# Attention decode with gradients on one core: dealing a head's cache rows to the partitions in another order, one transfer per head

## The chip, the core and the metric

The kernel runs on one core of a Trainium2 chip. TensorE (PE; its weight loads are listed as PEld), VectorE (DVE), ScalarE (ACT), GpSimd (POOL) and SyncE (SP) work side by side and meet through semaphores; 16 DMA engines carry data between HBM and the on-chip memory, whose 128 partitions hold the tiles. SP does no arithmetic here: it issues nearly all transfers, in the order written. The metric is the device time of one execution in microseconds.

## What is computed

A one-token attention step over a key and a value cache, mixed by a gate with a small dense network, and the gradients of the result by every input except the network's own (B_x). Sizes: D = 640, 32 heads of 128, 4096 cached positions, F = 1728, all in bf16.

```python
q = (x @ wq).reshape(1, 1, 32, 128)                 # one query per head
scores = einsum("bhqd,bhkd->bhqk", q, k_cache) * 128 ** -0.5
p = softmax(scores)
a = einsum("bhqk,bhkd->bhqd", p, v_cache).reshape(1, 1, 4096) @ wo
h = B_x @ w1 + b1
b = (h * tanh(softplus(h))) @ w2
g = sigmoid((x * gate_w).sum(-1))
out = g * a + (1 - g) * b
# returned: out and its gradients by x, k_cache, v_cache, wq, wo, w1, b1, w2, gate_w for grad_out
```

Each cache is 32 MB (32 heads x 4096 rows x 256 B). Both are read once, and a gradient of the same size is written for each. The gradient of a value row is the probability of its position times the head's output gradient; that of a key row is the score's gradient times the query. Softmax, sums and outer products run over a head's positions, and none of them depends on where a position stands.

## The kernel before

The heads are taken in 16 pairs (`NP`). For each pair `i` there is one tile of keys, `Kn`, and one of values, `Vn`: 128 partitions x 64 rows (`J`) x 128, 2 MB. Partitions 0 to 63 (`HP` = 64) hold the first head of the pair, 64 to 127 the second. The view at line 70 gives partition `a * 64 + q` the 64 consecutive cache rows of head `a` that begin at row `64 q`, which is one run of 16 KB in HBM. `load` (lines 106 to 111) brings such a tile with one DMA, or, for the first pair, with two DMAs of half of each partition's rows.

PE transposes the tiles (line 549, two bf16 values as one 32-bit word), ACT copies the transposes out of PSUM (line 560), and PE multiplies them with the query or the output gradient (line 575). From the row `x` (line 592) come scores and their gradients, with partition and row-in-partition as their two dimensions; maximum and sum over a head are taken across rows and the head's 64 partitions (lines 594 to 642). `dq_o` (line 675) goes through the natural tiles once more for the query's gradient and the head's output.

`out_part` (lines 651 to 666) makes a gradient tile on DVE in four outer products (`outer`, line 645, `JQ` = 16 rows of each partition at a time) and stores it: one DMA after the fourth (line 666), and for the first and the last pair one after every two (line 664). The tiles `o_sb` have two buffers, `Kn` and `Vn` two each; two of the last pairs' gradients go into `Kn` and `Vn` buffers that are no longer needed.

The order of the work is written out by hand, one engine's instructions in the order of the program: in step `i` the softmax of pair `i` runs, then transposes of pair `i + 1` between the outer products of pair `i`; the loads of pair `i + 2` are issued right after `dq_o(i)`, which is the last to read pair `i`. All these transfers are in SP's queue with the loads and stores of `wq` and `wo` (1280 KB for two groups of four heads and 640 KB for one; lines 129, 133, 415, 424) and of `w1` (lines 152, 887 and 888). `w2` is loaded and its gradient stored by an indirect DMA from POOL (lines 212 and 218) with one row of 20 KB for each of 108 partitions; the list `HOLES` names the 20 partitions that get none:

```python
HOLES = ((3, 5), (11, 13), (16, 20), (48, 52), (67, 69), (75, 77), (83, 85), (91, 93))
```

SP's DMAs use eight completion semaphores in turn, so each waits until the one eight before it has landed; a load waits besides for the last reader of its buffer, a store for DVE.

Of the kernel before, what the change touches and what calls it, by code (L numbers as in the profile page):

```python
# [16 lines left out]
def kernel(  # L17
# [24 lines left out]
    nc = tc.nc  # L42
    P = 128
    _, H, Sk, Dh = A_k_cache.shape
# [3 lines left out]
    J = 2 * Sk // P  # L48
    JU = J // 2
    NP = H // 2  # L50
    HP = P // 2
# [10 lines left out]
    for a, b in zip((0,) + tuple(b for a, b in HOLES), tuple(a for a, b in HOLES) + (P,)):  # L62
# [4 lines left out]
    TB = 8  # L67
    JQ = J // 4

    Kv, Vv, dKv, dVv = [t.rearrange("b (i a) (q j) d -> (b i) (a q) j d", a=2, j=J)  # L70
                        for t in (A_k_cache, A_v_cache, out_2, out_3)]
    wq_v = A_wq.rearrange("(rc r) c -> r rc c", r=P)
    dwq_v = out_4.rearrange("(rc r) c -> r rc c", r=P)
    wo4_v = A_wo.rearrange("(g p t) n -> g p t n", p=P, t=4)
# [31 lines left out]
    def load(tiles, src, name, i, parts=1):  # L106
        if i < NP:
            tiles[i] = kv_in.tile([P, J, Dh], BF16, name=name, tag=name)
            for k in range(parts):
                yield nc.sync.dma_start(tiles[i][:, k * J // parts:(k + 1) * J // parts, :],  # L110
                                        src[i][:, k * J // parts:(k + 1) * J // parts, :])

    def load_k(i):
        return list(load(kts, Kv, "Kn", i))

    def load_v(i):
        return list(load(vts, Vv, "Vn", i))
# [22 lines left out]
    dy_sb = mjunk[0:1, 0:D]  # L140
    nc.scalar.dma_start(dy_sb, dy_row)
    k0, v0 = load(kts, Kv, "Kn", 0, 2), load(vts, Vv, "Vn", 0, 2)
    next(k0)
    load_wqp(0)
# [499 lines left out]
    def outer(dst, col4, row, a, b):  # L644
        nc.vector.tensor_tensor(  # L645
            dst[:, a:b, :].rearrange("p j (k t) -> p j k t", t=4),
            row.rearrange("p (k t) -> p k t", t=4).unsqueeze(1).to_broadcast([P, b - a, Dh // 4, 4]),
            col4[:, a:b, :].unsqueeze(2).to_broadcast([P, b - a, Dh // 4, 4]), ALU.mult)

    o_t = {}  # L650

    def out_part(w, i, dst, col4, row, k):
        if k == 0:
            if w == "k" and i == NP - 2:
                o_t[w, i] = kv_in.tile([P, J, Dh], BF16, name="Kn", tag="Kn")
            elif w == "v" and i == NP - 1:
                o_t[w, i] = kv_in.tile([P, J, Dh], BF16, name="Vn", tag="Vn")
            else:
                o_t[w, i] = outs.tile([P, J, Dh], BF16, name="o_sb", tag="o_sb")
        outer(o_t[w, i], col4, row[:, i % 2 * Dh:(i % 2 + 1) * Dh], k * JQ, (k + 1) * JQ)  # L660
        if i in (0, NP - 1):
            if k % 2:
                js = slice((k - 1) * JQ, (k + 1) * JQ)
                nc.sync.dma_start(dst[i][:, js, :], o_t[w, i][:, js, :])
        elif k == 3:
            nc.sync.dma_start(dst[i], o_t.pop((w, i))[:])

    def dv_out(i, k):
        out_part("v", i, dVv, p4s[i], groups[i // 2]["do_row"], k)

    def dk_out(i, k):
        if i >= 0:
            out_part("k", i, dKv, ds4s[i], groups[i // 2]["qs_row"], k)
# [298 lines left out]
    g, i = NG - 1, NP - 1  # L972
# [102 lines left out]
```

## Time and profile before

| | |
|---|---|
| median of 3 runs | 405.23 us (404.2 to 407.51) |
| the profiled execution | 404.24 us, of which the profile's span is 402.4 |
| busy share of the span: PE, PEld, DVE, ACT, POOL | 73%, 51%, 69%, 56%, 7% |
| bytes moved | 164.54 MB, read and written in equal parts |
| SP's issues | 34 loads of `Kn` and `Vn` (30 of 2048 KB, 4 of 1024), 36 gradient stores (28 of 2048 KB, 8 of 1024), 27 others |
| granted TensorE clock, mean | 0.875 |

The page divides the span into 40 slices; a digit is the share of the slice in tenths. The DMA row is the mean over the 16 engines, and below it stand the GB/s that they moved. A packet is what an engine moves in one piece: for these tiles 16 KB, or 8 KB where a DMA takes half of each partition's rows. The trace also holds every packet's size and duration and the time of every semaphore increment; a DMA's completion semaphore goes up by 16, once for each DMA engine. The time to landing of a DMA is from its issue to the last of the 16.

### The profile page before, as it was taken

To read this page: it belongs to the slowest core of one execution; us is meant where nothing else is said; L and a number is where in the kernel's file an instruction comes from. 1 tells how busy PE (TensorE), PEld (TensorE's weight loads), DVE (VectorE), ACT (ScalarE), POOL (GpSimd) and SP (SyncE) were. 2 spreads that over 40 slices of the span, in tenths; PEclk is the share of its full clock that TensorE was granted. 3 is DMA by queue.
4 is the path that set the end of the run, shared out by engine and by line. 5 is a ranking of instruction groups with operands and counts; after the bars stand their busy time and mean duration, and the time that the engine had idled before them with its cause. 6 is when DMAs were issued, how large, how long until landed. Compare 5 with 4: busy or idle time off the path is not lost.

```text
span 402.4 us, 7413 instructions
## 1 busy us (share of the span) xinstructions
PE 294.7 (73%) x2886; PEld 204.3 (51%) x2886; DVE 278.7 (69%) x696; ACT 226.3 (56%) x484; POOL 27.5 (7%) x50
## 2 busy tenths in 40 slices
PE   3788889687859786685938887597957878396530
PEld 3556565465547463554626554464736655263220
DVE  3207257587849778877698957796697884459990
ACT  3465746577525955377445967659563865168030
POOL 9200005100000000000014000000000000010001
PEclk9898989999968999699979989689896999598555
DMA  7999999999999999999999999999999999999995
GB/s 273 433 420 416 420 415 433 417 422 396 428 377 401 385 416 430 421 417 430 427 430 428 420 417 429 405 423 423 430 413 393 425 415 430 401 425 428 397 419 226
DMA packets 20116, 164.54 MB, mean 409 GB/s; under 512 B 2456, under 2 KB 2457, under 8 KB 10905
## 3 DMA queue, kind: packets, MB, share of 16 engines
q1 hardware_dynamic: 18960, 159.62, 96.0%
q0 software_dynamic: 1088, 4.44, 2.7%
q8 instruction: 22, 0.36, 0.3%
q14 instruction: 14, 0.11, 0.1%
q10 hardware_dynamic: 32, 0.01, 0.0%
HBM read 82.44 MB, written 82.44 MB: 410 GB/s over the span
## 4 chain that ended last, share of the span: by engine, by line
DMA 53%; DVE 30%; PE 9%; ACT 4%; issue 2%; POOL 0%; POOLq 0%; ACTq 0%; DVEq 0%
DMA out_dram<-o_sb 51%; DVE o_sb L645 19%; PE tr L549 3%; ACT T L560 2%; DVE junk L508 1%; PE rw L575 1%; DMA Kn<-in_A_k_cache_dram 1%; DVE Vn L645 1%; DVE Kn L645 1%; DVE ds L637 1%; DVE junk L400 1%; DVE wq_p L410 1%; PE x L592 1%; PE do_ps L301 1%; PE mx L610 1%
## 5 line engine op out<-in xcount | busy, mean ns | idle before, releaser
L560 ACT COPY T<-tr 128x512 f32<-128x512 f32 x256 | 140.9, 592 | 108.8 <-PE tr L549 63.5
L549 PE MATMUL tr<-ident_f,Kn 128*128 128x128 f32 x512 | 85.0, 326 | 9.5 <-DMA Kn<-in_A_k_cache_dram 9.5
L645 DVE TENSOR_TENSOR o_sb<-do_row,p 128x2048 bf16<-128x2048 bf16 x60 | 69.4, 1219 | 29.7 <-DMA out_dram<-o_sb 29.7
L549 PE MATMUL tr<-ident_f,Vn 128*128 128x128 f32 x512 | 77.3, 284 | 12.4 <-ACT T L560 12.4
L549 PEld LDWEIGHTS tr<-ident_f,Kn 128*128 128x128 f32 x512 | 74.5, 174 | 16.1 <-issue 9.7
L645 DVE TENSOR_TENSOR o_sb<-qs_row,ds 128x2048 bf16<-128x2048 bf16 x60 | 73.0, 1223 | 13.3 <-DMA out_dram<-o_sb 13.3
L549 PEld LDWEIGHTS tr<-ident_f,Vn 128*128 128x128 f32 x512 | 54.4, 141 | 36.4 <-ACT T L560 22.3
L681 PE MATMUL rw<-Kn,dsm 128*8 128x512 bf16 x256 | 32.0, 394 | 3.4 <-DVE dsm L641 3.4
L681 PE MATMUL rw<-Vn,pm 128*8 128x512 bf16 x256 | 32.0, 394 | 0.0
L575 PE MATMUL rw<-T,doz 128*32 128x512 bf16 x256 | 21.2, 407 | 12.8 <-ACT T L560 12.8
L604 DVE TENSOR_REDUCE m<-sd 128x1 f32<-128x64 f32 x16 | 3.5, 216 | 32.2 <-ACT sd L599 32.2
L610 PE MATMUL mx<-ident_f,m_s 128*128 128x128 f32 x16 | 6.5, 408 | 25.6 <-DVE m_s L606 25.6
L400 DVE SCALAR_TENSOR_TENSOR junk<-wq_p,dq_bc 128x512 bf16<-128x512 bf16 x35 | 23.9, 684 | 0.0
L418 ACT ACTIVATE wo_g<-da_bc,o 128x640 bf16<-128x640 bf16 x28 | 23.8, 850 | 0.0
L592 PE MATMUL x<-ident_f,rw_sb 128*128 128x128 f32 x68 | 13.5, 331 | 13.0 <-ACT rw_sb L586 13.0
L575 PE MATMUL rw<-T,qz 128*32 128x512 bf16 x256 | 20.8, 401 | 0.2 <-ACT T L560 0.2
L592 PEld LDWEIGHTS x<-ident_f,rw_sb 128*128 128x128 f32 x68 | 8.6, 163 | 22.9 <-ACT rw_sb L586 22.9
L681 PEld LDWEIGHTS <-dsm 128*8 128x8 bf16 x256 | 11.1, 88 | 14.3 <-DVE dsm L641 8.2
L610 PEld LDWEIGHTS mx<-ident_f,m_s 128*128 128x128 f32 x16 | 2.6, 161 | 30.5 <-DVE m_s L606 30.5
L586 ACT COPY rw_sb<-rw 128x512 f32<-128x512 f32 x17 | 10.0, 591 | 11.2 <-PE rw L575 6.5
L599 ACT COPY sd<-x 64x128 f32<-64x128 f32 x32 | 8.3, 259 | 14.1 <-PE x L592 8.6
L516 POOL TENSOR_TENSOR mjunk<-ident_bf,dh_bf 128x96 bf16<-128x96 bf16 (+4 forms) x9 | 6.3, 728 | 136.3 <-DVE m L604 136.3
(183 smaller groups left out, 361.1 us busy)
## 6 DMA issues: line engine op xcount, KB each, us to landing
out_dram<-o_sb SPq DMA_DIRECT2D x27, 2048.0 KB, 14.7
Kn<-in_A_k_cache_dram SPq DMA_DIRECT2D x15, 2048.0 KB, 13.2
Vn<-in_A_v_cache_dram SPq DMA_DIRECT2D x15, 2048.0 KB, 17.6
out_dram<-o_sb SPq DMA_DIRECT2D x6, 1024.0 KB, 11.3
wq_p<-in_A_wq_dram SPq DMA_DIRECT2D x4, 1280.0 KB, 23.6
wo_g<-in_A_wo_dram SPq DMA_DIRECT2D x8, 640.0 KB, 20.2
out_dram<-wo_g SPq DMA_DIRECT2D x8, 640.0 KB, 12.8
out_dram<-wq_p SPq DMA_DIRECT2D x4, 1280.0 KB, 14.2
```

The costliest lines, as they stand in the source:

```text
L400: nc.vector.scalar_tensor_tensor(jq[:], in0=wqs[g][:, c, :], scalar=1.0, in1=groups[g]["dq_bc"][:], op0=ALU.mult, op1=ALU.mult, accum_out= ...
L418: nc.scalar.activation(wos[g][:, hh, :], da_bc[:], ACT.Copy, scale=groups[g]["o4"][:, hh:hh + 1])
L516: nc.gpsimd.tensor_tensor(mjunk[:, i * FCN:(i + n) * FCN].rearrange("p (a b) -> p a b", b=FCN), ident_bf[:, a:b].unsqueeze(2).to_broadcast ...
L549: nc.tensor.transpose(tp[:, t, :], words[:, t * P:(t + 1) * P], ident_f[:])
L560: nc.scalar.copy(TT[w, i, k][:, (3 - c) * (TB // 2):(4 - c) * (TB // 2), :], tp[:])
L575: nc.tensor.matmul(rw[32 * c:32 * (c + 1), :], lhsT=z[:, at:at + 32], rhs=Tb[:, c, par, :, :], start=first and par == 0, stop=last and par ...
L586: nc.scalar.copy(rw_sb[i][:].rearrange("p t r -> p (t r)"), rw[:])
L592: nc.tensor.transpose(xs[i][:, 3 - j, :], t[:, j, :], ident_f[:])
L599: nc.scalar.copy(sd[i][hs].rearrange("p s (k j) -> p k s j", k=2), v[hs, :, 8 + 4 * a:12 + 4 * a].rearrange("p j (k s) -> p k s j", k=2))
L610: nc.tensor.transpose(mx[:, 0:P], dgms.pop(i)[:].to_broadcast([P, P]), ident_f[:])
L645: nc.vector.tensor_tensor(dst[:, a:b, :].rearrange("p j (k t) -> p j k t", t=4), row.rearrange("p (k t) -> p k t", t=4).unsqueeze(1).to_br ...
L681: nc.tensor.matmul(rw[32 * c:32 * c + 8, :], lhsT=m[:, jb:jb + 4, :].rearrange("p q a -> p (q a)"), rhs=N[:, jb:jb + 4, :].rearrange("p j ...
```

## The change

Each head's 4096 rows are still cut into 64 runs of 64 rows (16 KB), one for each of the head's 64 partitions, but the runs are dealt in another order: partition `4 e + s` of a head (`e` from 0 to 15, `s` from 0 to 3) gets run `16 s + e`, where before partition `q` got run `q`. Four consecutive partitions thus hold runs that are 16 apart, and partitions 4 apart hold neighbouring runs. Keys, values and both gradients are dealt alike. A view with the pair's two heads in front would have needed one more dimension, so every transfer of a tile is made twice, once for each head: `flat` names the 64 partitions of a head in the tile, `dcols` the HBM side as 16 x 4 x bytes. The number of packets and their sizes stay, and no instruction on PE, DVE, ACT or POOL changes. SP issues 140 transfers of caches and gradients instead of 70.

```diff
-    Kv, Vv, dKv, dVv = [t.rearrange("b (i a) (q j) d -> (b i) (a q) j d", a=2, j=J)
+    Kv, Vv, dKv, dVv = [t.rearrange("b (i a) (s e j) d -> (b i) a e s (j d)", a=2, e=HP // 4, s=4)
                         for t in (A_k_cache, A_v_cache, out_2, out_3)]
+
+    def flat(t, a, js):
+        return t[a * HP:(a + 1) * HP, js, :].rearrange("p j d -> p (j d)")
+
+    def dcols(d, i, a, js):
+        return d[i, a, :, :, js.start * Dh:js.stop * Dh]
...
             for k in range(parts):
-                yield nc.sync.dma_start(tiles[i][:, k * J // parts:(k + 1) * J // parts, :],
-                                        src[i][:, k * J // parts:(k + 1) * J // parts, :])
+                js = slice(k * J // parts, (k + 1) * J // parts)
+                for a in range(2):
+                    nc.sync.dma_start(flat(tiles[i], a, js), dcols(src, i, a, js))
+                yield
...
             if k % 2:
                 js = slice((k - 1) * JQ, (k + 1) * JQ)
-                nc.sync.dma_start(dst[i][:, js, :], o_t[w, i][:, js, :])
+                for a in range(2):
+                    nc.sync.dma_start(dcols(dst, i, a, js), flat(o_t[w, i], a, js))
         elif k == 3:
-            nc.sync.dma_start(dst[i], o_t.pop((w, i))[:])
+            t = o_t.pop((w, i))
+            for a in range(2):
+                nc.sync.dma_start(dcols(dst, i, a, slice(0, J)), flat(t, a, slice(0, J)))
```

## The prediction, made before the changed kernel had run

> **What bounds the kernel now.** I read the page's slices first, since one core that moves 164.54 MB in 402.4 us is suspect of being bound by transfers, then the table of stretches, the chain of waits, the queues and issues, and last the trace's records of single packets and semaphore increments, which no view prints.
>
> The slices, the stretches (their columns: window, length, busy us of PE, PEld, DVE, ACT, POOL with counts, granted clock, DMA share, GB/s) and the chain:
>
> ```profile
> DMA  7999999999999999999999999999999999999995
> GB/s 273 433 420 416 420 415 433 417 422 396 428 377 401 385 416 430 421 417 430 427 430 428 420 417 429 405 423 423 430 413 393 425 415 430 401 425 428 397 419 226
> DMA packets 20116, 164.54 MB, mean 409 GB/s; under 512 B 2456, under 2 KB 2457, under 8 KB 10905
> q1 hardware_dynamic: 18960, 159.62, 96.0%
> ...
> DMA 53%; DVE 30%; PE 9%; ACT 4%; issue 2%; POOL 0%; POOLq 0%; ACTq 0%; DVEq 0%
> ```
>
> ```profile
> 40.00:200.00 160.00, 127.75 (x1333) 88.49 (x1331) 114.32 (x289) 94.17 (x206) 6.07 (x12) 0.94 1.01 415
> 200.00:360.00 160.00, 120.86 (x1165) 83.91 (x1163) 120.17 (x274) 99.35 (x209) 7.88 (x11) 0.87 1.01 419
> ```
>
> The DMA row is full in 38 of 40 slices, at 415 and 419 GB/s over the two middle stretches, while PE, DVE and ACT each have 32 us or more free in every 160. The best slices stand at 433 GB/s and none is above. The chain's other 47% is work between one transfer's end and the next issue; transfers already queued run beside it, or the DMA share would not be 1.01.
>
> ```profile
> out_dram<-o_sb SPq DMA_DIRECT2D x27, 2048.0 KB, 14.7
> Kn<-in_A_k_cache_dram SPq DMA_DIRECT2D x15, 2048.0 KB, 13.2
> Vn<-in_A_v_cache_dram SPq DMA_DIRECT2D x15, 2048.0 KB, 17.6
> ```
>
> A 2048-KB transfer follows its predecessor's landing by 4.9 us (K and V issued at 195.35 and 195.78 land at 208.54 and 213.42), so 14.7 us from issue to landing is about three tiles queued: the engines always have work waiting, and whatever makes a K/V transfer longer goes straight into the span.
>
> The packet records say what a packet costs. Median times are 84 ns for 2048 B, 196 for 5120, 309 for 8192, 611 for 16384, 761 for 20480 and 9 for the 4-B semaphore write. All six lie within 1 ns of 8 ns + bytes / 27.2 GB/s, loads and stores alike, in SP's queue and in POOL's. Of the 7,424 K/V packets of 16 KB 88% are within 1% of 611 ns. So each of the 16 engines runs at one fixed width, 27.2 GB/s, not at the pace of HBM.
>
> **The K/V share.** These 7,424 packets take 291.1 us of 16 engines' time and the 1,536 of 8 KB (pairs 0 and 15, moved in halves) 30.6: 321.7 us of the span are K/V traffic, of which only 7.6 + 0.9 = 8.5 us lie above the two medians.
>
> **The change, part by part.** *Order in HBM.* An engine's four rows of a head lie 256 KB apart instead of 16 KB, and what the 16 engines read at one time are 16 adjacent chunks instead of chunks 64 KB apart. Packets stay 16 KB (8 KB for the halves) with the same 8 ns each. The gain is bounded by the 8.5 us above the medians. The loss is bounded by the worst stretch of K/V packets, 110 to 120 us, at 376 GB/s against 16 x 611-ns packets' 429: if all K/V went so, 321.7 x (429/376 - 1) = 45 us. I take nothing: nine packets in ten have nothing to gain, and the neighbours of a chunk have no row that speaks against them.
>
> *More instructions.* 34 loads and 36 stores become 140, so 70 more issues at 0.34 us = 24 us on SP, which mostly waits (131 us for one kind of release alone) and has three tiles queued ahead; and 70 x 9 ns = 0.6 us of semaphore writes on each engine. SP reuses eight completion semaphores in turn, so a DMA waits for the landing of the one eight before it; eight half-tiles are still 8 MB, 19.5 us at the mean rate, against 14.7 us from issue to landing. Nothing is queued behind such a wait that the engines lack. PE's first transpose of a tile waits for two landings, both of which its one tile had before. DVE, ACT, POOL and PE keep their instructions; the sum over a head's rows does not care which partition has which row, since K, V, dK and dV are dealt alike. I take 0.6 us.
>
> *Half of the partitions at a time.* This decides. A tile's DMA has 128 partitions; now head 0's uses partitions 0 to 63, head 1's 64 to 127, one behind the other in the same queue. The trace of before has no big transfer on 64 partitions, so the price has two ends: nothing, if 27.2 GB/s is each engine's own width, or twice the time, if it is the width of the way into a group of partitions and two engines now share one. One transfer tells how partitions and engines belong together: the w2 load, whose row list leaves partitions 16 to 19 and 48 to 51 empty, and one or none of every other such 4 + 4. Of its 16 increments one comes 5.1 us before the next, the others lie within 1.9 us: one engine had nothing to do, so the blocks 16-19 and 48-51 are one engine's (seven to eight rows at 0.761 us are 5.3 to 6.1 us). Partitions 32 apart go to one engine, 64 apart to another: a division that looks like wiring, 16 ways of 27.2 GB/s with eight partitions each. A head on partitions 0 to 63 has eight of these ways, and if its 64 rows are dealt four to an engine, engines e and e + 8 meet in one. I take the upper end, because the constant is the same for both directions, both queues and all sizes, and the division follows the partitions.
>
> The Trainium skill's page "SBUF — State Buffer", section "Door 1: The DMA port swizzle (why `[64,N]` ≈ `[32,N]`)", says that partitions 0 to 63 reach eight of the 16 ports, and gives 196 GB/s against 328 for 1-MiB transfers on 64 and on 128 partitions; its next section adds that two transfers on the two halves don't overlap. By its ratio, 1.67, the K/V traffic would gain 216 us and the time be 620, an estimate from that page; no run here shows such a transfer yet.
>
> The sum by rows: at 13.6 GB/s a 16-KB packet takes 8 + 1205 = 1213 ns and an 8-KB one 610; 7,424 x 1213 / 16 + 1,536 x 610 / 16 = 562.8 + 58.6 = 621.4 us in place of 321.7: +300. The profiled execution took 404.2 (span 402.4 and 1.8 around it): 704. Two engines that meet lose less if one is ahead by part of a half tile (64 KB, 2.44 us). The tightest landing (the second half of K0) has all 16 within 0.40 us. The slowest pair sets when a buffer is released; pairs that gain a lead empty their queues, and both their engines start again together, so I take 0.1 us for it, 4% of 300, -12: 692 us, with 0.6 lost in rounding. The median of the three runs is 1.0 above the profiled one, too little to matter.
>
> **The rivals.** *Engines drift apart.* In mid-kernel the 16 landings of one DMA spread over 2 to 5 us (2.9 at 208.54, 5.7 at 345). If partners come to stand anywhere in the 4.9 us of a tile, they meet half of the time: +150, 555 us. For: the spread grows from 0.4 to over 5 us in the trace. Against: eight to ten of the 16 stay within 1 us, and one close pair is enough to hold the buffer. Between this and lockstep: 450 to 640.
>
> *The width is the engine's own.* Then nothing is lost; with 0.6 us of semaphores 405. For: the rate is the same whatever is moved. Against: so it would be with one way for each engine, and the w2 landings show engines tied to partitions.
>
> *Faster, by the order in HBM.* With the width the engine's own, the adjacent chunks could remove packets' excess: all of it gives 404.2 - 8.5 + 0.6 = 396, 2% faster. It decides from half of that on (4 us). For: the packets' excess is largest in 100 to 140 us, where hardly any other traffic runs, so it may be HBM's. Against: both conditions must hold, and there is little to win.
>
> *The order in HBM costs.* With the widths unshared, up to 45 us: 405 to 450, if chunks 256 KB apart on one engine slow it as packets in that worst stretch are slowed.
>
> **How the numbers follow.** Half ways in near lockstep 0.62 (640 to 740: partners 0.5 us apart take 20% off the 300; the top adds most of the 45 us); drift 0.18; order costs 0.05; no effect 0.06; faster 0.09. One per cent either way is about what a measurement of this kernel can tell from no change. Faster by over 1% is 0.09, within it 0.06, slower 0.85. The likeliest case alone ranges from 640 to 740; eight chances in ten need the drift as well, so 450 to 740.
>
> **What will show it.** In the changed kernel's slices DMA should stay at 9 with about 215 to 240 GB/s, PE and DVE digits falling to about half; 16-KB packets at 1.2 us rather than 0.61; issue to landing of a 1024-KB half no shorter than that of a whole tile now; wq and wo, still on 128 partitions, at their 84 and 196 ns unless they run beside a K/V packet. If packets mix 611 and 1213 ns, it is drift. If they stay at 611, the division into halves is free, and the sum's one large term is wrong; then the packets above 617 ns tell whether the order in HBM did anything.

## The result, and the profile after

The changed kernel takes 512.0 us (median of 4 runs, 504.8 to 517.7) against 404.7 for the kernel before (403.6 to 407.5): 1.247 times as long, 95% interval 1.240 to 1.254. That ratio counts only executions within 1.5% of their kernel's fastest, of the changed kernel those of 504.8 and 508.0 us; by the two medians it would be 1.265. Its profiled execution took 508.0 us, with a span of 506.3, 103.9 more than before.

The slices, the packets and the chain of waits of the changed kernel:

```profile
DMA  8999999999999899999999999999999999999994
GB/s 262 227 286 230 327 247 282 330 250 374 308 400 350 253 277 373 364 359 401 363 340 307 392 296 411 355 398 363 344 275 315 376 327 408 281 406 373 316 293 161
DMA packets 21236, 164.55 MB, mean 325 GB/s; under 512 B 3575, under 2 KB 3576, under 8 KB 12024
q1 hardware_dynamic: 20080, 159.62, 94.6%
...
DMA 65%; DVE 12%; PE 10%; SPq 6%; issue 2%; ACT 1%; ACTq 0%; POOLq 0%; POOL 0%; DVEq 0%
```

The DMA engines are as busy as before and carry a fifth less: 325 GB/s on average in place of 409. The bytes are the same, and the 1,120 additional packets are the 4-B semaphore writes (16 for each of 70 transfers). Two levels stand in the row: 227 to 330 in the first eight slices, then a restless 250 to 411. The table of stretches shows them in two lines (columns: window, length, busy us of PE, PEld, DVE, ACT, POOL with counts, granted clock, DMA share, GB/s):

```profile
20.00:110.00 90.00, 56.43 (x466) 38.97 (x466) 25.73 (x58) 35.49 (x78) 6.07 (x12) 0.77 1.02 276
110.00:480.00 370.00, 244.58 (x2376) 173.66 (x2374) 241.73 (x580) 184.48 (x393) 6.85 (x11) 0.80 0.99 348
```

Before, 20 to 110 us went at 419 GB/s and 110 to 380 at 416. The issues, with KB each and the median us to landing:

```profile
out_dram<-o_sb SPq DMA_DIRECT2D x54, 1024.0 KB, 19.1
Kn<-in_A_k_cache_dram SPq DMA_DIRECT2D x30, 1024.0 KB, 20.5
Vn<-in_A_v_cache_dram SPq DMA_DIRECT2D x30, 1024.0 KB, 22.3
```

Half a tile lands later than a whole one did. The packet records tell why. Of the 16-KB K/V packets 93% took up to 630 ns before; now 48% do, 13% take 1150 ns or more, and the rest lie between. From 65 to 110 us 4% take up to 630 ns and 61% 1150 or more, with a median of 1201 ns, which is the doubled packet; from 110 us on the median is 620. The K/V packets' time is 410.4 us of 16 engines' instead of 321.7 (+88.7), all packets' 495.2 instead of 399.2 (+96.0: the other packets take 7 us more too), and the rest of the 103.9 us, 8, is time in which engines had no packet.

### The profile page after: what moved, and what is told of

It is laid out like the page before. It is cut to its first block, busy times and chain, and to the rows that moved or that the text cites. A ratio compares the mean times of both kernels' runs of the same rounds, so it can differ in the third digit from the quotient of the medians.

```text
span 506.3 us, 7527 instructions
## 1 busy us (share of the span) xinstructions
PE 309.9 (61%) x2886; PEld 219.6 (43%) x2886; DVE 278.8 (55%) x696; ACT 226.9 (45%) x484; POOL 26.5 (5%) x50
## 4 chain that ended last, share of the span: by engine, by line
DMA 65%; DVE 12%; PE 10%; SPq 6%; issue 2%; ACT 1%; ACTq 0%; POOLq 0%; POOL 0%; DVEq 0%
DMA out_dram<-o_sb 32%; DMA Kn<-in_A_k_cache_dram 15%; DMA Vn<-in_A_v_cache_dram 14%; DVE o_sb L653 7%; PE tr L557 5%; SPq L141 5%; DMA out_dram<-Vn 2%; PE rw L692 2%; DVE junk L408 1%; DMA mjunk<-in_grad_out_dram 1%; PE rw L583 1%; DVE Kn L653 1%; SPq L118 1%; DVE Vn L653 1%; SPq L677 1%
## 5 line engine op out<-in xcount | busy, mean ns | idle before, releaser
L557 PE MATMUL tr<-ident_f,Kn 128*128 128x128 f32 x512 | 96.6, 356 | 42.6 <-DMA Kn<-in_A_k_cache_dram 41.0
L557 PEld LDWEIGHTS tr<-ident_f,Kn 128*128 128x128 f32 x512 | 83.7, 192 | 50.9 <-issue 48.7
L557 PE MATMUL tr<-ident_f,Vn 128*128 128x128 f32 x512 | 80.9, 295 | 17.8 <-ACT T L568 11.1
L557 PEld LDWEIGHTS tr<-ident_f,Vn 128*128 128x128 f32 x512 | 57.5, 147 | 42.7 <-ACT T L568 21.0
L632 DVE SCALAR_TENSOR_TENSOR pj<-sd,e_bf 128x64 f32<-128x64 f32 x16 | 4.3, 270 | 35.4 <-ACT e_bf L628 35.4
L376 ACT COPY wT<-tr 128x512 f32<-128x512 f32 (+1 forms) x27 | 14.4, 539 | 2.2 <-PE tr L370 2.2
L370 PE MATMUL tr<-ident_bf,wo_g 128*128 128x128 bf16 x160 | 13.5, 228 | 2.5 <-DMA wo_g<-in_A_wo_dram 2.5
## 6 DMA issues: line engine op xcount, KB each, us to landing
Kn<-in_A_k_cache_dram SPq DMA_DIRECT2D x30, 1024.0 KB, 20.5
out_dram<-o_sb SPq DMA_DIRECT2D x12, 512.0 KB, 13.6
```

The costliest lines, as they stand in the source:

```text
L370: nc.tensor.transpose(tp[:, t, :], src, ident_bf[:])
L376: nc.scalar.copy(wT[kind, g][:, k * TB:k * TB + n, :].rearrange("p a b -> p (a b)").bitcast(F32), tp[:, 0:n, :].rearrange("p a b -> p (a b ...
L557: nc.tensor.transpose(tp[:, t, :], words[:, t * P:(t + 1) * P], ident_f[:])
```

## The experiments

**One part alone: the halves, in the old order.**

```diff
-    ... t.rearrange("b (i a) (s e j) d -> (b i) a e s (j d)", a=2, e=HP // 4, s=4)
+    ... t.rearrange("b (i a) (e s j) d -> (b i) a e s (j d)", a=2, e=HP // 4, s=4)
```

> One transfer per head as in the changed kernel, but the runs dealt in the old order (partition q of a head has run q). Theory A, the halves: a transfer on 64 partitions reaches eight of 16 ways, in whatever order the runs lie in HBM: 500 to 520 us, packets of 16 KB at 1.2 us before 110 us as in the changed kernel. Theory B, the order in HBM: the old order is what the kernel before had, so 404 to 412 us with 16-KB packets at 611 ns. A mixture would lie between.

Measured: 559.6 us (555.1 to 564.5), before beside it 406.1. The halves alone cost more than the whole change. The new order does not cost anything; beside the halves it is worth some 48 us (559.6 against 512.0). The time lies above theory A's range of 500 to 520, which took the order for nothing. From 20 to 65 us 25% of the 16-KB packets take over 1300 ns here, 0.4% in the changed kernel.

**As many transfers, on all partitions.** Each transfer of the kernel before is cut along the rows of a partition.

```diff
+                w = J // parts // 2
-                yield nc.sync.dma_start(tiles[i][:, k * J // parts:(k + 1) * J // parts, :], ...)
+                for js in (slice(2 * k * w, (2 * k + 1) * w), slice((2 * k + 1) * w, (2 * k + 2) * w)):
+                    nc.sync.dma_start(tiles[i][:, js, :], src[i][:, js, :])
...
-            nc.sync.dma_start(dst[i], o_t.pop((w, i))[:])
+            for js in (slice(0, J // 2), slice(J // 2, J)):
+                nc.sync.dma_start(dst[i][:, js, :], t[:, js, :])
```

> The kernel before, each transfer cut in two along the rows of a partition: 140 transfers of 1 MB or 512 KB as in the changed kernel, all on 128 partitions, old order, packets of 8 KB. Theory A, the halves of the partitions: nothing but 8 ns for each of the 512 or so additional packets of an engine, +4 us: 407 to 413 us. Theory C, the number of transfers (SP's issues, the eight completion semaphores in turn): as slow as the changed kernel, 490 to 520 us.

Measured: 405.4 us, ratio to before 0.998 (0.995 to 1.001). Its page:

```profile
DMA packets 30198, 164.56 MB, mean 408 GB/s; under 512 B 3576, under 2 KB 3577, under 8 KB 15097
```

The number of transfers, of semaphore writes and of turns through the eight semaphores costs nothing that shows: theory C falls. The 4 us for smaller packets did not show in the time either; the K/V packets took 323.4 us in place of 321.7, 2 us more.

**Transfers alone.** Ten stages without computation; this kernel and the two further ones of transfers alone ran once each.

> Transfers alone, nothing of the reference is computed; ten stages, 32 MB each unless told, the queue emptied between them: (1) loads of whole tiles, (2) loads by heads, new order, (3) the same, old order, (4) all loads to partitions 0 to 63, (5) all loads to partitions 32 to 95, (6) as 2 behind a load that sets eight engines 64 KB back, (7) as 2 with the second head's loads from ACT's queue, (8) stores of whole tiles, (9) stores by heads, (10) stores from partitions 32 to 95. Theory A: 1, 5, 8 and 10 at 420 to 430 GB/s, 4 at 215, 2, 3 and 9 at 215 to 240 at their start and faster as they drift, 6 at 400 and more, 7 between. Theory B: 3 as 1, 2 slower than 3. Theory C: 2 to 5 alike, all slower than 1.

The stretches, inside the stages in the order of the text, stage 6 up to 720 us, stage 9 in two (columns: window, length, DVE and POOL busy, clock, DMA share, GB/s):

```profile
4.00:80.00 76.00, 7.73 (x16) 0.00 (x0) 1.00 1.01 430
88.00:238.00 150.00, 2.45 (x15) 0.00 (x0) 1.00 1.01 213
250.00:400.00 150.00, 2.44 (x15) 0.00 (x0) 1.00 1.01 212
410.00:560.00 150.00, 4.51 (x30) 0.00 (x0) 1.00 1.01 213
570.00:645.00 75.00, 4.56 (x30) 0.00 (x0) 1.00 1.01 428
652.00:720.00 68.00, 2.11 (x13) 0.00 (x0) 1.00 1.01 377
766.00:880.00 114.00, 2.28 (x14) 0.00 (x0) 1.00 1.01 241
892.00:962.00 70.00, 0.00 (x0) 0.00 (x0) 1.00 1.01 427
972.00:994.00 22.00, 0.00 (x0) 0.00 (x0) 1.00 0.99 315
994.00:1040.00 46.00, 0.00 (x0) 0.00 (x0) 1.00 1.01 429
1060.00:1130.00 70.00, 0.00 (x0) 0.00 (x0) 1.00 1.01 427
```

It is not 64 partitions that cost, but which: 0 to 63 give 213 GB/s, 32 to 95 give 428, with the same transfers of 1 MB. So two engines share a way, as the prediction's division has it. Loads by heads meet there from end to end, 213 and 212, in either order; they were expected to get faster as they drift, and in 150 us they don't. Stores by heads do: they are slow for some 22 us and then run at 429, although every transfer uses eight ways. A lead of 64 KB for eight engines takes loads from 213 to 377, and none of their packets from 652 to 720 us takes over 1045 ns; 400 and more was expected. (The queue was not empty between stages 6 and 7: nothing held back the loads from ACT's queue, whose first was issued at 719.85 us. What follows in stage 6 is a mixture.)

The semaphore records show what happened. These are the 16 increments of one load of stage 2 (issued at 114.67 us) and one store of stage 9 (issued at 1010.67), in us from the first of the 16:

```
load   0 .08 .09 .16 .21 .22 .23 .25 .26 .27 .28 .29 .30 .32 .33 .35
store  0 .27 .53 1.49 1.63 1.71 1.74 2.31 2.41 2.64 2.95 3.88 3.90 3.98 4.09 4.64
```

The load's engines land together. The store's come in eight couples 2.3 to 2.4 us apart (0 and 2.41, .27 and 2.64, .53 and 2.95, 1.49 and 3.88, ...). Half a tile is 2.44 us for an engine: of each couple one engine is at head 0 while the other is at head 1, and then each has a way to itself. That the couples are the engines that share a way is inferred; the records don't name engines.

The Trainium skill's page "SBUF — State Buffer", section "Can I just issue two DMAs to hit both halves?" (not the next section, as the prediction has it, but the one behind), says that they serialize. For loads the trace agrees, 213 against 430 GB/s; for stores it does not, 429 once the engines are apart, and there the measurement decides.

**Does phase decide inside the kernel?** The changed kernel with 0.5 MB more for eight engines, first at the start, then behind the loads of pair 1:

```diff
+    lead = outs.tile([P, J, Dh], BF16, name="o_sb", tag="o_sb")
+    nc.sync.dma_start(flat(lead, 0, slice(0, J))[0:32, :], dcols(Kv, 0, 0, slice(0, J))[0:8])
     k0, v0 = load(kts, Kv, "Kn", 0, 2), load(vts, Vv, "Vn", 0, 2)
```

> The changed kernel with one more load at the very start, 32 partitions dealt to eight engines only, 64 KB for each: these eight stand half a tile behind the other eight from then on. It leaves nothing out and adds 0.5 MB. If the loss is two engines meeting in one way (theory A) and goes as they drift apart, the slow first 110 us (276 GB/s from 20 to 110 us) become as fast as the rest or faster, 360 GB/s and more: 465 to 490 us. If phase does not matter and a way simply serves half the rate, the load is 1 to 3 us more: 510 to 520 us.

Measured: 518.4 us (507.0 to 523.0; the changed kernel 504.8 to 517.7), no gain. The first load of K0 landed on all 16 engines within 0.48 us: the lead was gone before anything could use it. This run does not test the phase, so it was moved:

> The changed kernel with the 0.5-MB load for eight engines behind the loads of pair 1, where tiles are queued, instead of at the very start, where nothing was queued behind it and the first pair's pieces are 32 KB, so that 64 KB are a whole period. If phase decides, the traffic from 60 to 110 us goes at 330 GB/s and more and the time falls to 470 to 500 us. If the 64 KB are lost again (by whatever sets partners back to the same place): 505 to 520 us.

Measured: 509.7 us (499.7 to 514.9), not clearly apart from 512.0 (504.8 to 517.7). From 65 to 110 us, the changed kernel and this one (its profiled execution took 508.5, near its median):

```profile
65.00:110.00 45.00, 26.00 (x211) 17.66 (x208) 15.85 (x37) 16.60 (x39) 6.07 (x12) 0.74 1.01 269
```

```profile
65.00:110.00 45.00, 30.91 (x256) 21.15 (x257) 17.92 (x45) 20.01 (x45) 6.07 (x12) 0.81 1.01 333
```

Where the lead was wanted it worked, 333 GB/s for 269 and 14% doubled packets for 61%. That is worth 45 x (333 - 269) / 400 = 7 us, by estimate, of which the added load takes 1 to 2; it does not last (342 GB/s from 110 to 480 us, 348 in the changed kernel), and the time hardly shows it. The expectation of 470 to 500 us was too much for a push at one place.

**Loads or stores alone by heads,** both in the old order, so that the other kind can be moved as whole tiles.

> Only the loads are made by heads (old order, so that whole tiles can be stored): beside 559 us with both by heads in this order. Theory D, loads meet in one way for good while stores set themselves apart: 67 MB at 212 instead of 421 GB/s are +157 us, and whole-tile stores set nothing apart: 520 to 565 us. Rival, loads and stores by heads cost alike: about half of the 153 us, 470 to 490 us.

Measured: 552.7 us, 1.357 times before (1.347 to 1.367): within theory D's range.

> Only the stores are made by heads (old order), loads on 128 partitions. Theory D: a store stream by heads is slow only until its engines are apart, 410 to 435 us. Rival, loads and stores by heads cost alike: 470 to 490 us.

Measured: 468.4 us, 1.155 times (1.148 to 1.163): far above theory D's range and just below the rival's. The rival's reason is not so either, since loads cost far more than stores. Stores inside the kernel do not run freely after a slow start. Whether they meet one another or the whole-tile loads between them is not shown: no stream mixed the two. The stretches of the loads' kernel, then of the stores':

```profile
20.00:110.00 90.00, 56.50 (x454) 37.86 (x452) 23.27 (x53) 33.94 (x73) 6.01 (x12) 0.76 1.02 256
110.00:520.00 410.00, 250.36 (x2307) 180.16 (x2307) 226.97 (x544) 184.12 (x388) 6.93 (x12) 0.76 0.99 304
```

```profile
20.00:110.00 90.00, 75.03 (x745) 51.24 (x744) 48.61 (x116) 54.19 (x119) 6.07 (x12) 0.96 1.01 398
110.00:440.00 330.00, 209.34 (x2076) 147.13 (x2070) 222.63 (x535) 164.47 (x350) 7.83 (x11) 0.81 0.98 355
```

Alone, loads cost 147 us and stores 63, together 153 (559.6): the parts don't add. That by-head stores also set the loads behind them apart would explain it; the next streams show that they can.

**Loads behind stores, and both orders.**

> Transfers alone, nothing of the reference is computed; seven stages, the queue emptied between them: (1) 32 MB of stores by heads, new order, (2) the same, old order, (3) 32 MB of stores, all from partitions 0 to 63, (4) 64 MB of whole tiles in the kernel's turn, K load, V load, two stores, (5) the same by heads, new order, (6) the same by heads, old order, (7) 8 tiles stored by heads and right behind them, without a pause, 16 tiles loaded by heads, new order. If stores set the two engines of a way half a tile apart by themselves: 1 near 295 GB/s at first, then 420 to 430, 3 at 215 from end to end, 4 at 410 to 425, 7 with loads at 350 and more at first, where loads alone ran at 212. If the order in HBM acts through that setting apart: 2 slower than 1, or 6 slower than 5 (330 GB/s in 5, 290 in 6). If the order acts on HBM itself, 2 is slower than 1 even in its last quarter.

Stage 3, then the mixture as whole tiles, by heads in the new order at its start and later, the same in the old order, and last the loads of stage 7:

```profile
192.00:345.00 153.00, 0.00 (x0) 0.00 (x0) 1.00 1.00 210
356.00:505.00 149.00, 2.62 (x16) 0.00 (x0) 1.00 1.01 427
516.00:560.00 44.00, 0.65 (x4) 0.00 (x0) 1.00 0.99 308
560.00:688.00 128.00, 1.96 (x12) 0.00 (x0) 1.00 1.01 401
695.00:740.00 45.00, 0.49 (x3) 0.00 (x0) 1.00 1.00 287
740.00:870.00 130.00, 1.96 (x12) 0.00 (x0) 1.00 1.01 395
...
915.00:1010.00 95.00, 2.28 (x14) 0.00 (x0) 1.00 1.00 376
```

Stores that all use partitions 0 to 63 have nowhere to evade to and stay at 210: so the 429 before came from the phase. Loads behind stores inherit the lead, 376 where loads alone had 213. The mixture starts slow and settles at 401. The order in HBM changes little here: stores alone go at 310, then 428 GB/s in the new order (stage 1) and at 318, then 428 in the old (stage 2), and the mixtures at 308 and 287 at the start, 401 and 395 later, 371 and 359 GB/s over the whole stages, 3%.

So free streams of both kinds come to 401, but the kernel to 348. One thing that differs is the waits.

> Transfers with the kernel's turn and its waits, nothing of the reference is computed: in each of 12 steps two loads wait for the buffers of two steps before, and two stores wait for some 7 us of DVE work each, which waits for the buffer's last store. 96 MB in each of five stages: (1) whole tiles, two buffers each, (2) by heads, new order, (3) by heads, old order, (4) as 2 with three buffers each, (5) as 2 without the DVE work. Stage 1 should stay above 400 GB/s. If the lead that engines gain is lost where the queue is short (a leading engine runs out of work and waits for its partner), 2 falls below the 371 GB/s of the ungated mixture, to 300 to 350, 4 and 5 rise above 2, and 3 is below 2 as 559 is behind 512 us. If waits do not matter, 2, 4 and 5 are alike at 360 to 380, and what holds the changed kernel at 355 GB/s is something else in it, such as its other transfers.

Of each stage behind the first, the slow start and the rest (the first line is stage 1, whole tiles):

```profile
30.00:230.00 200.00, 140.66 (x99) 0.00 (x0) 1.00 1.00 408
276.00:356.00 80.00, 28.92 (x22) 0.00 (x0) 1.00 1.01 253
356.00:560.00 204.00, 119.68 (x83) 0.00 (x0) 1.00 1.00 351
604.00:688.00 84.00, 28.93 (x22) 0.00 (x0) 1.00 1.01 239
688.00:890.00 202.00, 114.39 (x80) 0.00 (x0) 1.00 1.00 348
942.00:1020.00 78.00, 21.69 (x16) 0.00 (x0) 1.00 1.01 215
1020.00:1200.00 180.00, 113.45 (x80) 0.00 (x0) 1.00 1.01 383
1262.00:1340.00 78.00, 1.39 (x22) 0.00 (x0) 1.00 1.01 242
1340.00:1510.00 170.00, 4.46 (x80) 0.00 (x0) 1.00 1.01 409
```

With the kernel's two buffers and DVE work behind each store the mixture by heads settles at 351 GB/s, the changed kernel's 348. A third buffer each raises it to 383, no DVE work to 409, though the DMA share is 1.0 in all of them. The share of 16-KB packets with 1150 ns or more falls along: 8% (stage 2), 3% (stage 4), 0.3% (stage 5). So in the settled stretches the engines meet less where more work is queued. That with a short queue a leading engine runs out of work and waits for its partner is the likely way, but no record here names the engine that waits. Over whole stages the gain of the third buffer is small, since that stage starts at 215: with slow start and end, stages 2 to 5 go at 308, 299, 316 and 348 GB/s. A third buffer in the kernel itself wasn't tried.

An estimate from these rates comes near the changed kernel's K/V time: of its 134.2 MB, 20.2 in 80 us at 253 GB/s and 114.0 at 351 in 325 us make 405; its packets took 410.4. For the old order it fails: 239 and 348 GB/s make 412 us in the same way, where the K/V packets of the halves in the old order took 440.6. The streams don't show what the order is worth in the kernel.

## Why the prediction was wrong

*What bounds the kernel* was right: the transfers, before and after: of the span's additional 103.9 us, 96.0 are packets' time.

*The division of partitions into 16 ways* was right, down to the price of a meeting: 1201 ns for a packet in the slow stretch (forecast 1213), 213 GB/s for loads by heads (two packets of 16 KB on each way in 1213 ns would be 216), 428 on partitions 32 to 95.

*More instructions*, 0.6 us: right within what can be measured (0.998, 0.995 to 1.001). Eight half-tiles are 8.4 MB and take 20.5 us at the mean rate, not 19.5; nothing hangs on it.

*Order in HBM*, nothing: wrong in this company. Beside the halves the new order is worth some 48 us of the kernel's time, where the step took zero and bounded a gain by 8.5 us, a bound that counted only packets which met nobody. The streams by heads show the sign, 3%, not the size; where the rest comes from is open.

*The relief for engines that are not in step* is the step that failed, by size: the doubling of 300 us stood, and of it 4%, 12 us, was to be saved. K/V packets gained 88.7, so 211 us, 70%, were saved. The reason given was that one close pair holds every buffer and that leading pairs are started together again. Engines in step is what loads alone show (213 GB/s for 150 us without drift), though not why. Stores alone don't: they get the engines of a way half a tile apart within some 22 us, and loads queued behind them go on at 376 GB/s. That a short queue brings engines together again fits the streams with waits, but only in part: it left 351 GB/s, not 213. The rival *engines drift apart* is nearest to what happened; it had a chance of 0.18 and a price of 555 us, halfway, from chance positions. The changed kernel did better than that: 31% of the doubling is paid ((410.4 - 313.2) / 313.2, with 313.2 us for packets at their medians), not half. How the 70% divide among stores, loads behind them and the order in HBM is open. The trace of before had spoken for the rival, with a spread that grew from 0.4 to 5.7 us, and the sum had taken the tightest landing of all as typical.

*What will show it*: a mixture of 611 and 1213 ns was named as the mark of drift. The packets show it, with 38% between 630 and 1150 ns: as it would be with packets that meet another for a part of their time.

The 620 us by the Trainium skill's ratio of 1.67 were too many for the same reason: the ratio, put on all K/V traffic, has no term for engines that get apart.

## What to carry to other kernels

If a kernel is bound by transfers, each transfer should reach all 16 ways into the partitions: 64 partitions from 32 to 95 do (428 GB/s), 0 to 63 don't (213), and cutting a tile along its rows cost nothing here (405.4 us against 406.1). Where engines share a way, look at the phase of the engines before doubling the time: a packet's duration tells whether they meet, the 16 increments of a semaphore how far apart they are, and how much is queued bears on whether they stay so. A rearrangement that needs another form of transfer is two changes; each is to be priced and tried alone.

## What was not expected of the hardware

Loads by heads kept in step for 150 us at 213 GB/s, while stores by heads, through the same eight ways at a time, rose from 315 to 429 GB/s within 22 to 30 us. A lead of half a tile, given once, took the same loads to 377. Issued from two queues, one for each head, loads were hardly better, 241 GB/s. A full DMA share says nothing about the rate: it was 1.01 at 213 and at 430 GB/s.
